# A one-token attention decode on one core: 96 columns for 128 behind the values of three late sets, and the last two projection loads cut by partitions and heads

## The chip, the core and the metric

The kernel runs on one core of one Trainium2 chip. Five engines work side by side and meet at semaphores: TensorE (PE in the profile, with its weight loads as PEld), VectorE (DVE), ScalarE (ACT), GpSimd (POOL) and SyncE (SP), which here only issues transfers. Transfers themselves are carried out by 16 DMA engines. The metric is the device time of one execution in microseconds, a median over several; the profile is one execution taken by the hardware profiler.

## The reference

The input x is 8 tokens of 512 channels. Cut to what matters:

```python
xn = layernorm(x)                                  # no gain, no bias
q  = (xn @ wq)                                     # 8 x 32 heads x 128
k, v = k_cache[:, :, -1024:], v_cache[:, :, -1024:]   # window of 1024 of 4096 keys, 8 kv heads
o  = softmax(q k^T / sqrt(128)) v                  # 4 query heads share one kv head
s  = o.reshape(8, 4096) @ wo
g  = silu((gelu(xn @ w_gate) * (xn @ w_up)) @ w_down)
out = x + s * g
```

All matrices are bf16. The windows of keys and values are 16.8 MB each, and the weights add 13.9 MB (wq and wo 4.2 MB each).

## The kernel before, in words

**Sets.** One kv head of four batch entries is a set; there are 16 of them (`NQ`), sets 2h and 2h+1 belonging to kv head h. A set has 4 x 1024 keys, laid out as 32 chunks (`NCS`) of 128, and 16 query columns (`QC`, four heads by four entries). Its keys are one load of 1 MB, its values another (`load_set`, L122), into a ring of 16 buffers (`NRING`).

**Transfers.** All loads are issued by SP in one order (L176 to L189): the feed-forward weights, wq, the keys of four sets, then for each set q the keys of set q+4 and the values of set q; behind every second set comes `load_wo`, the four heads of the output projection that belong to that kv head, 512 KB as rows of 1 KB (128 partitions, four heads). The values of the last set are loaded as 768 KB and 256 KB. The order at the end is therefore values 12, values 13, projection 24 to 27, values 14, values 15 in two parts, projection 28 to 31. In the built program SP's loads take eight semaphores in turn, and each waits until the load that used its semaphore before, the eighth before it, has landed; a load into the ring also waits until its buffer was read.

**Order on TensorE.** The program is written in a fixed order (L536 to L560). Each step of the loop over q does four quarters `i`, each with eight chunks: transposes of keys two quarters ahead, the values of the set five steps back (`v = q - LAG`), the scores of set q. In between stand the largest score of the set before (`max_all`, L440), which VectorE turns into a shift (L442, L447, L450), and the matmul that subtracts it (`exponentials`, L461), and behind it the exponential on ScalarE (L470). Steps 16 to 20 have no keys any more: they hold the values of sets 11 to 15 alone, with two heads of `project` (L526, four matmuls a head) behind each of the later two quarters at every second step. The four heads 28 to 31 come after the loop (L563), then the gate (L566), four transposes (L569), the sum with x (L571) and the store (L572).

**Values.** `values(g)` (L492) does eight of the 32 chunks of a set. Each matmul takes one chunk of values as weights and the exponentials of that chunk as moving data. It writes `wide` groups of 16 columns: only the first group, the chunk's own, is ever read, and the others are the following chunks' columns, multiplied with the wrong values and left alone. The accumulator `o_ps` has one buffer, so the values of a set start after `normalise` (L511) of the set before has read it.

```python
            wide = VCW if NQ - LAG <= q < NQ - 2 else VC
            wide = wide if n + wide <= NCS else 1
            nc.tensor.matmul(
                o_ps[q][:, 0:wide, :],
                v_sb[q][n],
                pT[q][:, n : n + wide, :],
```

`VC` is 4 (64 columns) and `VCW` is 8 (128 columns); the wide form is used in sets 11, 12 and 13. Where fewer than `wide` chunks are left the matmul has 16 columns.

Of the kernel before, what the change touches and what calls it, by code (L numbers as in the profile page):

```python
# [17 lines left out]
def kernel(  # L18
# [35 lines left out]
    nc = tc.nc  # L54
# [3 lines left out]
    Hkv, Sk, Dh = A_k_cache.shape[1], A_k_cache.shape[2], A_k_cache.shape[3]  # L58
    Hq = A_wq.shape[1] // Dh
    rep = Hq // Hkv  # L60
# [3 lines left out]
    P = nc.NUM_PARTITIONS  # L64
# [9 lines left out]
    NCS = QG * NSC  # L74
    VC = 4
    SC = 8
    VCW = 8
    NRING = 16
    MASK = -1.0e30
    NG = Hkv * B  # L80
    NQ = NG // QG
# [8 lines left out]
    weights = ctx.enter_context(tc.tile_pool(name="weights", bufs=1))  # L90
    ring = ctx.enter_context(tc.tile_pool(name="ring", bufs=NRING))
    consts = ctx.enter_context(tc.tile_pool(name="consts", bufs=1))
# [20 lines left out]
    wo_sb = weights.tile([P, Hq, D], BF16, name="wo_sb")  # L113
# [50 lines left out]
        )  # L164

    def load_wo(hkv):
        nc.sync.dma_start(
            out=wo_sb[:, hkv * rep : (hkv + 1) * rep, :],
            in_=A_wo[hkv * rep * Dh : (hkv + 1) * rep * Dh, :].rearrange(
                "(k p) d -> p k d", p=P  # L170
            ),
        )


    nc.scalar.dma_start(out=x_sb, in_=A_x.flatten_outer_dims())
# [8 lines left out]
    for q in range(NQ):  # L184
        if q + LEAD < NQ:
            load_k(q + LEAD)
        load_v(q)
        if q % SH == SH - 1:
            load_wo(q // SH)  # L189
# [7 lines left out]
        out=ident,  # L197
        in_=ident,
# [14 lines left out]
        out=row_of,  # L213
        in_=row_of,
# [6 lines left out]
    other = consts.tile([QG, QG, rep], BF16, name="other")  # L221
    nc.vector.memset(other, MASK)
    nc.gpsimd.affine_select(
        out=other,
        in_=other,
# [21 lines left out]
    for i in range(2):  # L247
# [3 lines left out]
            out=t[MK : MK + QG, :], in_=other.rearrange("g s j -> g (s j)")  # L251
# [5 lines left out]
        out=spread[MK : MK + QG, :], in_=row_of.rearrange("g e s -> g (e s)")  # L257
# [7 lines left out]
    def keep_busy(n):  # L265
# [12 lines left out]
        out=rstd, in_=mv[:, 1:2], func=ACT.Sqrt, bias=eps_sb, scale=1.0  # L278
# [4 lines left out]
        out=xhat,  # L283
# [208 lines left out]
    def values(g):  # L492
        q, i = divmod(g, NB)
        if i == 0:
            o_ps[q] = ps_o.tile([P, VCW, QC], FP32, name="o_ps")
        for c in range(NSC):
            n = i * NSC + c
            wide = VCW if NQ - LAG <= q < NQ - 2 else VC
            wide = wide if n + wide <= NCS else 1
# [103 lines left out]
```

## Time and profile before

| what | value |
|---|---|
| time, median of 3 runs | 125.16 us (124.97 to 125.5) |
| the profiled execution's own time | 125.26 us |
| its span, first to last instruction | 123.5 us |
| PE busy, share of the span | 107.2 us, 87% |
| DVE busy | 63.3 us, 51% |
| ACT busy | 44.6 us, 36% |
| bytes moved, mean rate | 47.76 MB, 387 GB/s |
| mean granted TensorE clock | 0.986 |

Times in the profile are microseconds from the first instruction. The chain of work that ended last goes back from the last instruction to what released it, or to the instruction before on the same engine. In the chain, a line gives start, length and what ran. In the stretches, each line gives a stretch, its length, the busy time of each engine with its number of instructions, the granted clock, the busy share of the 16 DMA engines and the rate in GB/s. The time from issue to landing of a load is counted from the start of the issue by SP to its last completion event; a load has one such event for each DMA engine that carries a part of it, and a queued load spends most of that time behind the loads before it.

### The profile page before, as it was taken

To read this page: it belongs to the slowest core of one execution; us is meant where nothing else is said; L and a number is where in the kernel's file an instruction comes from. 1 tells how busy PE (TensorE), PEld (TensorE's weight loads), DVE (VectorE), ACT (ScalarE), POOL (GpSimd) and SP (SyncE) were. 2 spreads that over 40 slices of the span, in tenths; PEclk is the share of its full clock that TensorE was granted. 3 is DMA by queue.
4 is the path that set the end of the run, shared out by engine and by line. 5 is a ranking of instruction groups with operands and counts; after the bars stand their busy time and mean duration, and the time that the engine had idled before them with its cause. 6 is when DMAs were issued, how large, how long until landed. Compare 5 with 4: busy or idle time off the path is not lost.

```text
span 123.5 us, 4657 instructions
## 1 busy us (share of the span) xinstructions
PE 107.2 (87%) x2118; PEld 90.0 (73%) x2123; DVE 63.3 (51%) x189; ACT 44.6 (36%) x54; POOL 1.2 (1%) x7
## 2 busy tenths in 40 slices
PE   0999999998999999999999779794999698979980
PEld 0366557456689888899989678793999687868970
DVE  3700001200046888898877576673478385673431
ACT  4000003200027877756655635352536364401000
POOL 3000000000000000000000000000000000000000
PEclk9999999999999999999999999999599999999999
DMA  3999999999999999999999999999999999999600
GB/s 95 413 420 429 426 422 424 424 435 430 416 427 416 432 400 425 422 427 394 434 424 415 418 427 414 414 416 424 419 409 426 424 407 417 415 408 409 237 22 3
DMA packets 10468, 47.76 MB, mean 387 GB/s; under 512 B 832, under 2 KB 4944, under 8 KB 5968
## 3 DMA queue, kind: packets, MB, share of 16 engines
q1 hardware_dynamic: 10432, 47.46, 93.5%
q8 instruction: 16, 0.26, 0.8%
q14 instruction: 4, 0.03, 0.1%
q10 hardware_dynamic: 16, 0.01, 0.0%
HBM read 47.46 MB, written 0.01 MB: 384 GB/s over the span
## 4 chain that ended last, share of the span: by engine, by line
PE 53%; DMA 31%; DVE 10%; issue 4%; POOLq 0%; POOL 0%; ACT 0%; DVEq 0%
DMA ring_sb<-in_A_k_cache_dram 31%; PE idle_ps L267 15%; PE kT_ps L404 10%; PE o_ps L500 8%; PE gu_ps L306 5%; PE sc_ps L421 4%; PE qT_ps L381 3%; PE sc_ps L461 3%; DVE mx L432 2%; DVE kT L411 2%; PE sT_ps L526 1%; PE aux_ps L474 1%; DVE diag L450 1%; DVE diag L447 1%; DVE nm L442 1%
## 5 line engine op out<-in xcount | busy, mean ns | idle before, releaser
L404 PE MATMUL kT_ps<-ident,ring_sb 128*128 128x128 bf16 x512 | 39.6, 221 | 4.8 <-DMA ring_sb<-in_A_k_cache_dram 4.6
L413 ACT COPY kT<-kT_ps 128x1024 bf16<-128x1024 bf16 x32 | 32.4, 1012 | 25.0 <-PE kT_ps L404 24.7
L404 PEld LDWEIGHTS <-ring_sb 128*128 128x128 bf16 x512 | 30.5, 98 | 8.0 <-DMA ring_sb<-in_A_k_cache_dram 5.1
L411 DVE COPY kT<-kT_ps 128x1024 bf16<-128x1024 bf16 x32 | 22.0, 688 | 7.0 <-PE kT_ps L404 6.7
L500 PE MATMUL o_ps<-pT,ring_sb 128*128 128x64 bf16 (+2 forms) x512 | 25.4, 195 | 0.2
L421 PE MATMUL sc_ps<-qT_all,kT 128*128 128x16 bf16 x512 | 22.4, 170 | 1.2 <-ACT pT L470 0.8
L500 PEld LDWEIGHTS <-ring_sb 128*128 128x128 bf16 x512 | 22.3, 99 | 1.1 <-issue 1.0
L267 PE MATMUL idle_ps<-ones_w 128*128 128x512 bf16 x53 | 20.3, 528 | 0.7 <-issue 0.5
L421 PEld LDWEIGHTS <-kT 128*128 128x128 bf16 x512 | 19.3, 96 | 1.8 <-ACT pT L470 0.9
L470 ACT ACTIVATE pT<-sc_ps 128x512 bf16<-128x512 f32 x16 | 9.6, 597 | 18.8 <-PE sc_ps L461 18.8
L432 DVE TENSOR_REDUCE mx<-sc_ps 128x16 f32<-128x512 f32 x16 | 11.1, 692 | 2.6 <-PE sc_ps L421 2.4
L267 PEld LDWEIGHTS <-ones_w 128*128 128x128 bf16 x58 | 6.0, 120 | 7.4 <-issue 6.2
L511 DVE TENSOR_TENSOR oT_all<-o_ps,recip 128x16 bf16<-128x16 f32 x16 | 3.7, 228 | 12.6 <-PE o_ps L500 12.6
L306 PEld LDWEIGHTS <-ring_sb 128*128 128x128 bf16 x112 | 7.5, 161 | 1.8 <-issue 1.8
L306 PE MATMUL gu_ps<-xnT_sb,ring_sb 128*128 128x8 bf16 x112 | 7.2, 201 | 0.3 <-DVE xnT_sb L295 0.3
L461 PE MATMUL sc_ps<-diag,spread 68*128 68x512 bf16 x16 | 6.0, 376 | 1.5 <-DVE diag L450 1.5
L323 DVE TENSOR_SCALAR z<-z 128x112 f32<-128x112 f32 x1 | 0.2, 219 | 13.5 <-ACT z L320 13.5
L526 PE MATMUL sT_ps<-oT_all,wo_sb 128*128 128x8 bf16 x128 | 5.7, 167 | 1.0 <-issue 0.5
L526 PEld LDWEIGHTS <-wo_sb 128*128 128x128 bf16 x128 | 4.9, 97 | 2.2 <-issue 1.6
L474 PE MATMUL aux_ps<-pT,ones_pp 128*128 128x128 bf16 x64 | 6.4, 224 | 0.0
L320 ACT ACTIVATE z<-gu_ps 128x112 f32<-128x112 f32 x1 | 0.3, 265 | 14.8 <-PE gu_ps L306 14.8
L442 DVE TENSOR_REDUCE nm<-aux_ps 16x1 f32<-16x128 f32 x16 | 4.4, 276 | 2.1 <-PE aux_ps L440 1.3
(57 smaller groups left out, 54.3 us busy)
## 6 DMA issues: line engine op xcount, KB each, us to landing
ring_sb<-in_A_k_cache_dram SPq DMA_DIRECT2D x16, 1024.0 KB, 19.2
ring_sb<-in_A_v_cache_dram SPq DMA_DIRECT2D x15, 1024.0 KB, 18.9
ring_sb<-in_A_wq_dram SPq DMA_DIRECT2D x4, 1024.0 KB, 18.9
wo_sb<-in_A_wo_dram SPq DMA_DIRECT2D x8, 512.0 KB, 17.7
ring_sb<-in_B_w_gate_dram SPq DMA_DIRECT2D x2, 896.0 KB, 6.7
ring_sb<-in_B_w_up_dram SPq DMA_DIRECT2D x2, 896.0 KB, 6.7
ring_sb<-in_B_w_down_dram SPq DMA_DIRECT2D x2, 896.0 KB, 12.1
ring_sb<-in_A_v_cache_dram SPq DMA_DIRECT2D x1, 768.0 KB, 14.9
```

The costliest lines, as they stand in the source:

```text
L267: nc.tensor.matmul(idle_ps, ones_w[:, 0:P], ones_w, start=True, stop=True)
L306: nc.tensor.matmul(ffn["gu"][:, j, n % 2, :], up_sb[n][:, i, j::NFC], xnT_sb[:, k, :], start=(n == 0 and j == 0 and i == 0), stop=(k == ND ...
L404: nc.tensor.transpose(kT_ps[:, c * P : (c + 1) * P], k_sb[q][n], ident,)
L411: nc.vector.tensor_copy(out=kT[g], in_=kT_ps)
L413: nc.scalar.copy(out=kT[g], in_=kT_ps)
L421: nc.tensor.matmul(sc[q][:, i * NSC + c, :], kT[g][:, c * P : (c + 1) * P], qT_all[:, b : b + QG, hkv * rep : (hkv + 1) * rep], start=(i = ...
L432: nc.vector.tensor_reduce(out=mx, in_=sc[q].rearrange("p c n -> p n c"), axis=AX.X, op=ALU.max)
L461: nc.tensor.matmul(sc[q], spread, shift[q].unsqueeze(1).to_broadcast([MK + QG, NCS, QC]), start=False, stop=True, skip_group_check=True,)
L470: nc.scalar.activation(out=pT[q], in_=sc[q], func=ACT.Exp, scale=inv_sqrt_dh)
L474: nc.tensor.matmul(sums_ps, ones_pp, pT[q][:, c * SC : (c + 1) * SC, :], start=(c == 0), stop=(c == NCS // SC - 1),)
L500: nc.tensor.matmul(o_ps[q][:, 0:wide, :], v_sb[q][n], pT[q][:, n : n + wide, :], start=(n == 0), stop=(n == NCS - 1), skip_group_check=True,)
L526: nc.tensor.matmul(sT_ps[0][:, d, :], wo_sb[:, h, d * P : (d + 1) * P], oT_all[:, h, :], start=(h == 0 and d == 0), stop=(h == Hq - 1), sk ...
```

## The change

Two things are changed. `VCW` goes from 8 to 6: the values of sets 11, 12 and 13 are multiplied with six chunks of exponentials (96 columns) beside a chunk of values, and the accumulator `o_ps` has six groups. As six chunks fit behind 27 of the 32 chunks and eight behind 25, a set has 27 wide matmuls and 5 of 16 columns in place of 25 and 7.

`load_wo` cuts its last two loads. That of heads 24 to 27 becomes two: partitions 0 to 107, and partitions 108 to 127, each with four heads. That of heads 28 to 31 becomes four: heads 28 to 30 in the same two parts, then head 31 in the same two parts. The bytes are the same. SP issues 55 loads in place of 51, and behind the first part of projection 24 to 27 each load takes another of the eight semaphores, so that it waits for another load than before: the second part waits for keys 14, values 14 for values 10 where it waited for keys 14, the parts of values 15 for keys 15 and values 11 where they waited for values 10 and keys 15, and the four last parts for projection 20 to 23, values 12, values 13 and the first part of projection 24 to 27. The order of instructions on the other engines is the same.

```diff
-    VCW = 8
+    VCW = 6
     NRING = 16
+    CUTS = (0, 108, P)
...
     def load_wo(hkv):
-        nc.sync.dma_start(
-            out=wo_sb[:, hkv * rep : (hkv + 1) * rep, :],
-            in_=A_wo[hkv * rep * Dh : (hkv + 1) * rep * Dh, :].rearrange(
-                "(k p) d -> p k d", p=P
-            ),
-        )
+        h0, h1 = hkv * rep, (hkv + 1) * rep
+        heads = (h0, h1) if hkv < Hkv - 1 else (h0, h1 - 1, h1)
+        cuts = CUTS if hkv >= Hkv - 2 else (0, P)
+        for a, z in zip(heads, heads[1:]):
+            rows = A_wo[a * Dh : z * Dh, :].rearrange("(k p) d -> p k d", p=P)
+            for p0, p1 in zip(cuts, cuts[1:]):
+                nc.sync.dma_start(out=wo_sb[p0:p1, a:z, :], in_=rows[p0:p1, :, :])
```

## The prediction

> **What bounds the kernel now.** I read the profiled execution first by its overview, then by the chain that ended last, then the end by stretches and by its loads. The overview names TensorE, but 87% is a mean over stages:
>
> ```profile
> span 123.5 us, 4657 instructions
> PE 107.2 (87%) x2118; PEld 90.0 (73%) x2123; DVE 63.3 (51%) x189; ACT 44.6 (36%) x54; POOL 1.2 (1%) x7
> GB/s 95 413 420 429 426 422 424 424 435 430 416 427 416 432 400 425 422 427 394 434 424 415 418 427 414 414 416 424 419 409 426 424 407 417 415 408 409 237 22 3
> ```
>
> Rates stay near 420 GB/s until the 37th of 40 slices: there the loads set the pace. The chain shows where that ends:
>
> ```profile
> 83.13 18.51 DMA ring_sb<-in_A_k_cache_dram
> 101.64 0.05 issue
> 101.69 0.62 PE kT_ps L404 x8
> ...
> 109.46 0.89 PE o_ps L500 x16
> 110.35 0.12 PE aux_ps L440
> 110.48 0.02 issue
> 110.50 0.29 DVE nm L442
> ...
> 111.35 0.38 PE sc_ps L461
> 111.72 0.23 PE o_ps L500 x8
> ...
> 112.26 1.50 PE o_ps L500 x24
> ...
> 114.61 1.61 PE o_ps L500 x32
> ...
> 118.23 0.96 PE o_ps L500 x32
> 119.19 0.02 issue
> 119.22 0.24 DVE oT_all L511
> 119.45 0.04 issue
> 119.49 0.56 PE sT_ps L526 x16
> 120.07 0.20 DVE sg L566
> ```
>
> The last keys land at 101.64. From there no load stands in the chain: TensorE works through scores and values, with VectorE's short links between. So a nanosecond saved on TensorE after 101.7 counts, as long as the last loads keep ahead. These are stretches of the end (behind the five engines' busy times: granted clock, DMA share, GB/s) and the last load's size and time to landing:
>
> ```profile
> 114.00:115.00 1.00, 1.00 (x30) 1.00 (x27) 0.54 (x3) 0.00 (x0) 0.00 (x0) 1.00 0.98 375
> 116.00:117.00 1.00, 0.92 (x29) 0.80 (x27) 0.71 (x3) 0.00 (x0) 0.00 (x0) 1.00 0.52 180
> 118.00:119.00 1.00, 1.00 (x35) 1.00 (x34) 0.60 (x3) 0.00 (x0) 0.00 (x0) 1.00 0.04 15
> wo_sb<-in_A_wo_dram SPq DMA_DIRECT2D x1, 512.0 KB, 13.8
> ```
>
> The clock is full. The transfers thin out from 115 on because the DMA engines end apart. The last load is issued at 104.87, so it lands at 118.6-118.7, and its sixteen completion events stand in two groups: nine at 114.9 to 116.4, then 117.8, four at 117.9, 118.2 and 118.6. Its weights are wanted at 119.49: 0.9 us of slack. The cause of the two groups is in the trace's packets: sixteen instruction fetches of 16 KB (about 0.93 us each, with a slow packet behind each), and followed back to back through the packets, eight DMA engines got two each, the other eight none.
>
> **The wide values.** The starts of successive matmuls in sets 11 to 15 stand 55.7 ns apart at 128 columns, 29.2 at 64, 25.3 at 16. Ninety-six columns are not in the trace; they lie between 29.2 and 55.7, and I take the middle, 42.4, since from 64 to 128 a column costs 26.5/64 = 0.414 ns and 2.4 columns a nanosecond fits the full clock.
>
> - Set 13 (and set 12 alike): before 25 x 55.7 + 7 x 25.3 = 1570 ns; after 27 x 42.4 + 5 x 25.3 = 1271. Saved 0.299 us each, all on the chain.
> - Set 11: its first 16 matmuls stand ahead of the transpose of L440, which moves up by 16 x 13.3 = 0.213 us; its operand was ready at 109.29, 0.9 us before it ran. From it the chain goes through VectorE (L442, L447, L450) to L461, 111.35, with TensorE idle for 0.44 us: what the next eight save (0.107) falls into that wait. The last eight are three wide and five narrow in place of one and seven: 254 for 233 ns, 0.021 lost. Saved 0.192.
> - Sum 0.299 + 0.299 + 0.192 = 0.79 us. Bounds: at 29.2 each it would be about 1.7, at 55.7 a loss of 0.06 a set, 0.18 together.
>
> What is late next: the values of set 14 would start at 116.53 - 0.79 = 115.74 (landed 114.8), the first part of values 15 at 117.32 (116.6), chunk 24 at 118.02 (117.3), head 28 at 118.70 (118.6). Head 31 follows twelve matmuls of 25.3 later, at 119.00. So the loads cap the gain near 0.8, even at the cheap bound.
>
> **The divided loads.** The bytes stay; no load stood in the chain after 101.64, so an earlier landing is worth nothing by itself, and what counts is whether head 31's last piece lands after 119.00 and heads 28 to 30 after 118.70. Kilobyte packets start 42.7 ns apart on one DMA engine (32 of them 1.37 us, as the first engine's events at 113.5 and 114.9 show). How 108 and 20 rows fall on the engines is not in the trace: 128 rows give sixteen events, the 8 rows of x eight packets. Bounds: an even share (8 rows an engine as before) lands at 118.6, plus four completion packets of 9 ns; a share on eight engines as for x (16 rows each, 32 more packets in both loads, 2 x 1.37 us) lands at up to 121.3 if late engines are among them. I take a landing of at most 119.0: 108 rows are nearer to 128 than to 8. The cost is then zero, under the cover of the values of sets 14 and 15.
>
> [...]
>
> **Queues.** SP's four more issues cost it under 2 us each (1.33 and 1.64 us for the undivided), and it then waits until 121.18 anyway. Values 14 would be issued once values 10 landed (99.2) in place of 96.83; the first engines reach it at 108.6. Head 31's last piece waits for the first part of projection 24 to 27 (about 112.3), and with an issue and the 1.3 us from issue to landing of the output store it could land from 115; the quickest engines come to it at about 115.5. What covers these is up to 10 us of data queued in front; if that is gone, the piece is late, as in the third rival. Nothing but the store is queued behind it on SP.
>
> **Sum.** The profiled execution took 125.26 us, 123.5 in the span and 1.7 around it, 0.1 above the median of 125.16. 125.26 - 0.79 = 124.47; from the median, 124.4.
>
> **Rivals.**
> - *No change: the pieces fall on the late engines.* [...] For it: half of the engines are late, and which carry which rows the trace does not tell. [...]
> - *Slower: few engines.* The counts seen are 16 and 8; on four engines both pieces split evenly (27 and 5 rows), 96 more packets in each load. Then even a quick engine ends at 115.4 + 8.2 = 123.6 in place of due 119.0: about 129. On eight engines with late ones, 121.3, head 31 1.5 us later than before: 126.7. It decides from a last landing of 119.79, where head 31 begins now. Against: only the smallest load ran on fewer than sixteen.
> - *Slower: each piece pays its own start.* [...] As a mechanism here: three further pieces at the store's 1.3 us in series bring the last landing to 118.6 + 3.9 = 122.5, about 127.9. Against: queued loads follow without a gap (113.5 and 114.9 above are 32 packets apart).
> - *No gain from 96 columns:* at 55.7 a matmul, 125.16 + 0.18 = 125.3. Against: 64 columns do cost less.
>
> **How the numbers follow.** Forecast 124.4 (124.2 to 124.7) 0.58; late engines, 125.1, 0.22; few engines 0.08; piece starts 0.03; dear columns 0.06; the rest 0.03 in between. About 0.5% (0.63 us) is what a measurement of this kernel tells from no change, 124.53 here, and the forecast's own range reaches over it, so 0.04 of it goes to no change: faster 0.54, same 0.35 (with the late engines, the dear columns and the rest), slower 0.11. The range 124.1 to 125.4 takes in the forecast, the late engines and the dear columns; the slower rivals are left out.
>
> **What would show it.** In the changed profile: sets 12 and 13 about 0.3 us shorter each and their matmuls 42 ns apart; L461 of the last set at about 111.1; oT_all of set 15 at 118.4 in place of 119.22; the completion events of the divided loads fewer than 16 and, for head 31, none after 119.0; no DMA in the chain after 101.7. It is wrong if the chain holds wo_sb at its end, or if a wait of values 14 or 15 for its load appears.

## The result: slower by 3.3 us

The changed kernel takes 128.62 us in the median (128.1 to 128.96) against 125.3 us (124.97 to 125.5) for the kernel before: a ratio of 1.0247, 95% interval 1.0206 to 1.0288. The prediction had 124.4, in a range of 124.1 to 125.4. Executions over 1.5% above the fastest of their kernel are left out of the ratios and intervals, here and below, but not out of the medians: the 128.24 us below, for only heads 24 to 27 cut, has one of 168.1 us in it.

The profiled execution of the changed kernel has a span of 126.4 us where the kernel before had 123.5. Its overview, with the granted clock in tenths and the rate by slices:

```profile
span 126.4 us, 4669 instructions
PEclk9995555799999999999999986999999689999855
GB/s 96 415 429 422 428 420 441 417 425 420 433 415 428 428 405 417 423 409 420 428 428 395 430 420 417 418 425 417 411 419 428 419 411 423 268 273 338 195 61 3
```

Up to the 34th slice (107 us) the rates are those of before. Then there are three slices of 268, 273 and 338 GB/s where the kernel before has 415, 408 and 409 in its 35th to 37th slice, so the bytes come in later. (The clock of 0.5 between 10 and 23 us costs nothing: in this stage TensorE waits for weights, and the last keys land at 101.8, where they landed at 101.6 before.)

The end of the chain of the changed kernel, start and length:

```profile
102.76 17.30 DMA ring_sb<-in_A_v_cache_dram
120.06 0.05 issue
120.11 1.81 PE o_ps L504 x32
...
121.94 0.24 DVE oT_all L515
...
122.22 0.58 PE sT_ps L530 x16
...
122.83 0.20 DVE sg L570
...
123.07 0.60 PE sg_ps L573 x4
```

A load now stands in the chain: the 768 KB part of the values of set 15. The timeline of TensorE shows the waits for the values in brackets (start, length, instruction, idle time before it and what ended it):

```profile
114.03 1.42 PE L504 MATMUL o_ps<-pT,ring_sb 128*128 128x96 bf16 x32
116.59 0.40 PE L478 MATMUL aux_ps<-pT,ones_pp 128*128 128x128 bf16 x4 [1.14 <-DVE oT_all L515]
117.50 0.87 PE L504 MATMUL o_ps<-pT,ring_sb 128*128 128x64 bf16 x24 [0.51 <-DMA ring_sb<-in_A_v_cache_dram]
...
120.11 1.80 PE L504 MATMUL o_ps<-pT,ring_sb 128*128 128x64 bf16 x32 [0.87 <-DMA ring_sb<-in_A_v_cache_dram]
```

TensorE comes earlier, as forecast: set 13 begins at 114.03 in place of 114.49, and its 32 matmuls stretch over 1.42 us in place of 1.72. But the values of set 14 land at 117.4 (114.8 before, wanted at 115.74), the two parts of the values of set 15 at 120.1 and 120.8 (116.6 and 117.3; wanted at 117.32 and 118.02), and the last projection piece at 122.3 (118.6; wanted at 119.00). What ended the 1.14 us ahead of L478 is not settled; the values behind it were not there before 117.4 anyway.

Against the forecast span of 123.5 - 0.79 = 122.7: set 15 starts at 120.11 in the chain in place of 118.23 - 0.79 = 117.44 (2.67 us); its matmuls take 1.81 us in place of 0.96 (0.85), and the last matmuls and transposes 0.22 more. With 0.11 less around the store that is the difference of 3.63 us between the two spans.

The stretches in which the bytes were lost (behind the five engines' busy times: granted clock, busy share of the DMA engines, GB/s). First the kernel before:

```profile
108.00:111.00 3.00, 2.39 (x52) 2.17 (x48) 2.08 (x7) 0.38 (x1) 0.00 (x0) 1.00 1.04 417
111.00:114.00 3.00, 2.58 (x52) 2.33 (x52) 1.03 (x5) 0.60 (x1) 0.00 (x0) 1.00 1.02 409
```

Then the changed kernel:

```profile
108.00:111.00 3.00, 2.54 (x62) 2.24 (x61) 2.14 (x8) 0.60 (x1) 0.00 (x0) 1.00 1.04 262
111.00:114.00 3.00, 2.76 (x65) 2.52 (x65) 1.11 (x5) 0.60 (x1) 0.00 (x0) 1.00 1.08 276
117.00:119.00 2.00, 1.50 (x52) 1.51 (x52) 0.73 (x3) 0.00 (x0) 0.00 (x0) 1.00 0.86 221
```

The DMA engines are as busy as before (1.04 and 1.08, against 1.04 and 1.02) and move a third less (262 and 276 GB/s, against 417 and 409). In the trace's packets it is not the new pieces alone that are slow: from 107.7 to 114.3 us packets of 8 KB, which belong to the undivided values, take 414 to 558 ns in the medians by microsecond in place of 309, and kilobyte packets 53 to 72 in place of 46. Between 115 and 116.5 both are back at 309 and 46, and from 117 to 119.2, with the last four pieces in flight, kilobyte packets stretch again (medians of 67 and 58 ns) and so do the 6 KB packets of the values of set 15 (399 and 315 in place of 234). This points to a collision of transfers, which the experiments test. The completion events also show how the rows fall: twelve for 108 rows and ten for 20, besides one at the issue.

### The profile page after: what moved, and what is told of

Same layout as the page of the kernel before. It is cut to its first block, busy times and chain, and to the rows that moved or that the text cites. A ratio compares the mean times of both kernels' runs of the same rounds, so it can differ in the third digit from the quotient of the medians.

```text
span 126.4 us, 4669 instructions
## 1 busy us (share of the span) xinstructions
PE 108.2 (86%) x2123; PEld 91.1 (72%) x2123; DVE 63.2 (50%) x189; ACT 44.6 (35%) x54; POOL 1.2 (1%) x7
## 4 chain that ended last, share of the span: by engine, by line
PE 44%; DMA 43%; DVE 8%; issue 2%; POOLq 0%; POOL 0%; ACT 0%; DVEq 0%; SPq 0%
DMA ring_sb<-in_A_k_cache_dram 30%; PE idle_ps L271 14%; DMA ring_sb<-in_A_v_cache_dram 14%; PE kT_ps L408 9%; PE gu_ps L310 5%; PE o_ps L504 4%; PE sc_ps L425 3%; PE qT_ps L385 3%; DVE mx L436 2%; DVE kT L415 2%; PE sc_ps L465 2%; PE fT_ps L349 1%; PE sT_ps L530 1%; DVE diag L454 1%; DVE diag L451 1%
## 5 line engine op out<-in xcount | busy, mean ns | idle before, releaser
L408 PE MATMUL kT_ps<-ident,ring_sb 128*128 128x128 bf16 x512 | 40.2, 224 | 6.1 <-DMA ring_sb<-in_A_k_cache_dram 6.1
L408 PEld LDWEIGHTS <-ring_sb 128*128 128x128 bf16 x512 | 31.0, 99 | 9.2 <-DMA ring_sb<-in_A_k_cache_dram 6.7
L504 PEld LDWEIGHTS <-ring_sb 128*128 128x128 bf16 x512 | 22.5, 102 | 2.7 <-DMA ring_sb<-in_A_v_cache_dram 1.7
L310 PEld LDWEIGHTS <-ring_sb 128*128 128x128 bf16 x112 | 7.5, 161 | 1.6 <-issue 1.3
L478 PE MATMUL aux_ps<-pT,ones_pp 128*128 128x128 bf16 x64 | 6.7, 231 | 1.1 <-DVE oT_all L515 1.1
L465 PE MATMUL sc_ps<-diag,spread 68*128 68x512 bf16 x16 | 6.0, 376 | 1.6 <-DVE diag L454 1.6
L486 DVE TENSOR_REDUCE recip<-aux_ps 128x16 f32<-128x128 f32 x16 | 4.5, 284 | 1.8 <-PE aux_ps L478 1.8
```

The lines of the kernel that those rows point to most:

```text
L310: nc.tensor.matmul(ffn["gu"][:, j, n % 2, :], up_sb[n][:, i, j::NFC], xnT_sb[:, k, :], start=(n == 0 and j == 0 and i == 0), stop=(k == ND ...
L408: nc.tensor.transpose(kT_ps[:, c * P : (c + 1) * P], k_sb[q][n], ident,)
L465: nc.tensor.matmul(sc[q], spread, shift[q].unsqueeze(1).to_broadcast([MK + QG, NCS, QC]), start=False, stop=True, skip_group_check=True,)
L478: nc.tensor.matmul(sums_ps, ones_pp, pT[q][:, c * SC : (c + 1) * SC, :], start=(c == 0), stop=(c == NCS // SC - 1),)
L504: nc.tensor.matmul(o_ps[q][:, 0:wide, :], v_sb[q][n], pT[q][:, n : n + wide, :], start=(n == 0), stop=(n == NCS - 1), skip_group_check=True,)
```

## The experiments

The theories at first: **L** (lanes): rows that do not fall on the DMA engines as 128 rows do make engines collide. **U** (unequal shares): twelve and ten engines carry what sixteen did. **S** (small pieces): the number of loads and their semaphores. All edits are given against the changed kernel, but for the last one under "Which partitions belong to an engine", which is against the kernel just ahead of it. The bytes loaded are the same in every kernel here, but for the two with further loads, which load 768 KB more.

| kernel | median, us | beside it, kernel before | ratio, 95% interval |
|---|---|---|---|
| changed | 128.62 | 125.3 | 1.0247, 1.0206 to 1.0288 |
| six chunks alone | 124.7 | 125.32 | 0.9951, 0.9926 to 0.9976 |
| division alone | 128.81 | 125.32 | 1.0260, 1.0193 to 1.0327 |
| six chunks, last load by heads alone | 124.67 | 125.32 | 0.9935, 0.9896 to 0.9975 |
| cut at 96 | 127.95 | 125.32 | 1.0186, 1.0132 to 1.0239 |
| whole, source rows 768 bytes apart | 124.63 | 125.58 | 0.9908, 0.9867 to 0.9948 |
| cut at 64, every second source row | 128.36 | 125.58 | 1.0217, 1.0144 to 1.0289 |
| cut at 120 | 127.71 | 125.58 | 1.0173, 1.0096 to 1.0251 |
| only heads 24 to 27 cut at 108 | 128.24 | 125.58 | 1.0162, 1.0059 to 1.0264 |
| only heads 28 to 31 cut at 108 | 125.45 | 125.32 | 0.9986, 0.9955 to 1.0018 |
| further loads into partitions 0 to 31 | 127.18 | 125.32 | 1.0133, 1.0076 to 1.0190 |
| further loads into partitions 64 to 95 | 134.34 | 125.32 | 1.0704, 1.0641 to 1.0766 |
| four chunks, last load by heads alone | 124.48 | 125.32 | 0.9918, 0.9881 to 0.9955 |

### The two parts alone

```diff
-    CUTS = (0, 108, P)
+    CUTS = (0, P)
...
-        heads = (h0, h1) if hkv < Hkv - 1 else (h0, h1 - 1, h1)
+        heads = (h0, h1)
```

> The six chunks alone, loads undivided. All theories say that the columns are worth what the prediction had for them: about 0.8 us, 124.3 to 124.7, with the last projection load landing at 118.6 just ahead of need. If the columns themselves were to blame for the loss, it stays at 128 or more.

Measured: 124.7, ratio 0.9951, a gain of 0.6 us (0.3 to 0.9), within the expectation. The columns are not to blame.

```diff
-    VCW = 6
+    VCW = 8
```

> The division alone, eight chunks as before. If the loads alone make the loss, the values of set 15 land at 120.1 as in the changed kernel, whatever TensorE does before, and the time is 128.1 to 129. If the loss needs both parts (TensorE reaching its loads earlier), it is near 125.3.

Measured: 128.81, the loss of the changed kernel within its interval. The end of this kernel's chain:

```profile
101.86 16.75 DMA ring_sb<-in_A_v_cache_dram
118.61 0.05 issue
118.66 1.31 PE o_ps L504 x24
...
121.16 1.49 PE o_ps L504 x32
```

The chain runs through the values of set 14 here, and TensorE never waits for set 15, whose parts land at 120.9 and 121.5: with eight chunks and a granted clock of 0.5 from 118.9 us on it comes later. The expectation that the values of set 15 land at 120.1 and set the end was too narrow; that the division alone makes the loss stands.

### Pieces, shares or places

Last load by heads alone, and the cut moved to where both parts fall evenly on sixteen engines:

```diff
-    CUTS = (0, 108, P)
+    CUTS = (0, P)
```

> Six chunks, and the last load divided by heads alone (three heads, one head), each piece with all 128 partitions. Theory L (lanes: rows that do not fall on the DMA engines as 128 rows do make engines collide, and every packet in flight takes longer): packets stay at 309 and 46 ns, 124.3 to 124.7. Theory U (unequal shares of the engines): the same. Theory S (small pieces and their semaphores): about half of the loss, 126 or more.

```diff
-    CUTS = (0, 108, P)
+    CUTS = (0, 96, P)
```

> Divided as in the changed kernel but at partition 96: 96 and 32 rows fall evenly on sixteen engines (six and two rows each). Theory L: the rows stand in other places than the same engine's rows of a 128-row load, so 8 KB packets stretch from 309 to 450 ns or more while the pieces run, and the time is 127 to 129. Theory U: even shares, no loss, 124.3 to 124.8. Theory S: as the changed kernel, 128.

Measured: 124.67 with the pieces by heads, their packets at 46 and 309 ns; 127.95 with the cut at 96, 8 KB packets at 444 to 556 ns in the medians between 108 and 115 us. Theory U falls with the second: both parts have sixteen completion events each there (six and two rows an engine), and the time is 3.3 us over that of the kernel divided by heads alone; with nine and two rows on twelve and ten it is 4.0 us over (128.62). Theory S missed with the first, but that kernel has one further piece where the changed one has four, so it tests S in part; the pair of kernels with further loads, below, shows the loss with the number of loads equal. The stretches of the kernel divided by heads alone:

```profile
108.00:111.00 3.00, 2.38 (x58) 2.08 (x55) 2.24 (x8) 0.54 (x1) 0.00 (x0) 1.00 1.04 413
111.00:114.00 3.00, 2.92 (x72) 2.71 (x71) 1.10 (x5) 0.60 (x1) 0.00 (x0) 1.00 1.01 407
```

and of the kernel cut at 96:

```profile
108.00:111.00 3.00, 2.59 (x62) 2.37 (x62) 1.84 (x7) 0.60 (x1) 0.00 (x0) 1.00 1.04 249
111.00:114.00 3.00, 2.37 (x54) 2.02 (x52) 1.31 (x6) 0.60 (x1) 0.00 (x0) 1.00 1.02 264
```

### Reading side or writing side

A divided load changes both what an engine reads and where it writes. One kernel changes only the distance between the source rows. The other changes the partitions and takes every second source row, meant to keep the engines' sources as far apart as before:

```diff
-    CUTS = (0, 108, P)
+    CUTS = (0, P)
...
+            if hkv >= Hkv - 2:
+                rows = bass.AP(A_wo.tensor, a * Dh * D, [[384, P], [Dh * D, z - a], [1, D]])
```

> Undivided partitions, the last load in two by heads as in the kernel divided by heads alone; the rows of the last two loads are read 768 bytes apart in place of 1024, so that sixteen engines read 6 KB apart, as with the cut at 96 (heads 24 to 31 get wrong weights: the last two loads' contents are left out of the computation, their sizes are the same). Theory LS (the collision is on the reading side, by the distance between the engines' addresses): packets stretch as with the cut at 96, about 128. Theory LD (it is on the writing side, by the partitions that an engine writes): 46 and 309 ns, 124.3 to 124.9.

```diff
-    CUTS = (0, 108, P)
+    CUTS = (0, 64, P)
...
-                nc.sync.dma_start(out=wo_sb[p0:p1, a:z, :], in_=rows[p0:p1, :, :])
+                step = P // (p1 - p0)
+                first = p0 * step // P
+                nc.sync.dma_start(out=wo_sb[p0:p1, a:z, :], in_=rows[first:P:step, :, :])
```

> Cut at partition 64: both halves on sixteen engines, four partitions each, and every second row of the source, so that the engines read 8 KB apart as in the undivided load (heads 24 to 31 get their rows in another order: those weights are left out of the computation, sizes the same). Theory LD: packets stretch, 126.5 to 130. Theory LS: 46 and 309 ns, 124.3 to 124.9.

Measured: 124.63 and 128.36. The stretch of the first:

```profile
108.00:111.00 3.00, 2.48 (x54) 2.33 (x51) 1.61 (x5) 0.60 (x1) 0.00 (x0) 0.78 1.01 403
```

and of the second:

```profile
108.00:111.00 3.00, 2.67 (x62) 2.30 (x61) 2.08 (x8) 0.60 (x1) 0.00 (x0) 1.00 1.05 263
```

This speaks for the writing side: source rows 768 bytes apart do no harm (403 GB/s), and halves of 64 partitions do, though their source rows are spread (263 GB/s). It does not settle it, because the distances of 6 and 8 KB in the expectations take the rows of an engine to be neighbours, which the next kernel speaks against. What settles it is the pair behind that one, whose further loads read the same source.

### Which partitions belong to an engine

```diff
-    CUTS = (0, 108, P)
+    CUTS = (0, 120, P)
```

> Cut at partition 120: 120 rows divide by fifteen, eight rows an engine, 8 rows by eight. If an engine's partitions in a 128-row load are eight in a row, the first fifteen engines write where they always do, and only the small piece is out of place: little loss, 124.4 to 125.5. If an engine's partitions in a 128-row load are not eight in a row, it is as bad as the others, 127 to 129.

Measured: 127.71, as bad as expected for partitions that are not eight in a row. That left the place of writing to test by itself, with undivided partitions: the kernel with six chunks and the last load divided by heads alone, and behind the projection loads of kv heads 1, 3 and 5 one further load of 256 KB into a tile that nothing reads. Two kernels write these bytes, from the same source and in the same split (eight completion events each), into two places, partitions 0 to 31 and 64 to 95.

```diff
-    CUTS = (0, 108, P)
+    CUTS = (0, P)
...
+    NP = 4096
+    probe = weights.tile([P, NP], BF16, name="probe")
...
+        if hkv in (1, 3, 5):
+            nc.sync.dma_start(
+                out=probe[0:32, :],
+                in_=bass.AP(A_wo.tensor, 0, [[4 * NP + D, 8], [NP, 4], [1, NP]]),
+            )
```

> [...]

```diff
-                out=probe[0:32, :],
+                out=probe[64:96, :],
```

> [...]

Measured: 127.18 and 134.34, 7.2 us apart for a change of the partitions alone. With partitions 0 to 31, from 25 us on 4062 of 4081 packets of 8 KB take 309 to 313 ns; with 64 to 95, 356 of 4083 take 420 to 700 ns, all of them in three stretches (57 to 63, 82 to 90 and 108 to 116 us), one for each further load. A stretch at the first of them, with partitions 0 to 31:

```profile
57.00:61.00 4.00, 4.00 (x102) 3.76 (x100) 3.31 (x11) 2.53 (x3) 0.00 (x0) 1.00 1.04 424
```

and with partitions 64 to 95, ahead of it, in it and behind it:

```profile
53.00:57.00 4.00, 4.00 (x102) 3.76 (x97) 3.35 (x10) 2.53 (x4) 0.00 (x0) 1.00 1.01 414
58.00:61.00 3.00, 3.00 (x76) 2.76 (x73) 2.35 (x8) 2.16 (x3) 0.00 (x0) 1.00 1.07 237
62.00:66.00 4.00, 2.02 (x47) 1.69 (x44) 1.82 (x7) 1.01 (x1) 0.00 (x0) 1.00 0.98 406
```

So the place that is written decides: source, bytes and split are the same. The stretch at the first load into partitions 64 to 95 lasts some 4 us (58 to 62). The loads into partitions 0 to 31 stretch no packets, but cost time too, 127.18 us against 124.67 without them: the last pieces' completion events are three at 115.2 to 116.4, then a group at 117.9 to 119.9, then 121.4 and 121.5. Eight engines got three times four packets of 8 KB more, which start 306 ns apart in the trace of the kernel before, by estimate 3.7 us. This fits two late engines among the eight (117.8 + 3.7 = 121.5); then the late engines are not simply the other eight.

No trace here names the DMA engine of a packet, so which partitions an engine writes in a 128-row load is not shown, nor why one place is slow and the other not. Shown is that 32 partitions from 0 on stretch nothing, that 32 from 64 on stretch every 8 KB packet that began between 58 and 62 us (97 packets, the least 448 ns), and that 120 rows, by their events on fifteen engines, with the other 8 on eight, take the rate to 288 GB/s between 108 and 111 us.

### Where in the changed kernel

```diff
-        cuts = CUTS if hkv >= Hkv - 2 else (0, P)
+        cuts = CUTS if hkv == Hkv - 2 else (0, P)
```

> Only the load of heads 24 to 27 divided at 108; the last one by heads alone. In the changed kernel packets are stretched twice, from 107.7 to 114.5 and from 117 to 119.5. Theory L in either form: the first stretch stays, the values of set 15 land at about 119 and the time is 127 to 128. If the loss came mostly from the four last pieces, it is under 125.5.

```diff
-        cuts = CUTS if hkv >= Hkv - 2 else (0, P)
+        cuts = CUTS if hkv == Hkv - 1 else (0, P)
```

> Only the last load divided at 108 (and by heads), the load of heads 24 to 27 whole. Packets stretch only from about 114 on, when most of values 15 is in. If the loss follows the data still in flight beside the pieces, it is small: 124.7 to 126. If each divided load costs the same, half of the loss: 126.5.

Measured: 128.24 with the first load divided (about 127.6 by the ratio), and 125.45 with the last. Against 124.67 without a cut, the last load's pieces cost about 0.8 us and the first's the greater part, though its interval is wide (1.0162, 1.0059 to 1.0264) and only its times are shown here, not its packets. With only the last one divided, 8 KB packets stay at 309 up to 114 us, and the end waits for the pieces themselves, in the chain of that kernel:

```profile
106.00 13.43 DMA wo_sb<-in_A_wo_dram
119.43 0.14 issue
119.57 0.44 PE sT_ps L530 x12
```

That the loss follows the data in flight beside the pieces fits both times.

### Fewer columns still

```diff
-    VCW = 6
+    VCW = 4
...
-    CUTS = (0, 108, P)
+    CUTS = (0, P)
```

> Four chunks (64 columns) in all sets, no cut by partitions, last load in two by heads: TensorE would save 1.7 us against the kernel before, but the last loads land at 118.6 as before and hold the end: 124.2 to 124.6, no more than 0.4 better than six chunks with the same loads (124.67).

Measured: 124.48, ratio 0.9918 (0.9881 to 0.9955). It is faster than the kernel before, by under 1%, and than the changed kernel; from six chunks with the same loads (0.9935, 0.9896 to 0.9975) it can't be told apart. In its chain TensorE waits 0.22 us behind the matmuls of set 13, where the kernel with six chunks and the same loads has 0.02; what it waits for the profile does not show:

```profile
114.02 0.94 PE o_ps L504 x32
114.97 0.22 issue
115.18 0.40 PE aux_ps L478 x4
```

## Why the prediction was wrong

- **The wide values: right.** Matmuls of ninety-six columns stand 42.3 ns apart at a granted clock of 1.00 (42.4 predicted, the middle of 29.2 and 55.7), set 13 went from 1.61 to 1.31 us on the chain where no load is late (in the kernel divided by heads alone), and the six chunks alone gained 0.6 us (0.3 to 0.9) where 0.79 was forecast. L461 of the last set, L465 in the changed kernel, came at 111.16, predicted 111.1.
- **The divided loads: the step that failed.** "The cost is then zero, under the cover of the values of sets 14 and 15." Both bounds counted packets at 42.7 ns and asked only how many an engine gets. The price of the packet itself changed, for all loads in flight: the 127 packets of 8 KB that began between 108 and 114 us took 381 to 605 ns, in the median 509, where all took 309 in the kernel before. What I named as cover was the victim: the values of sets 14 and 15 came 2.6 and 3.5 us later, and TensorE waited for them, which was my own sign of being wrong. The bound of 121.3 for the last landing was passed as well (122.3).
- **The rival of few engines** named times on both sides of the measured one (126.7 and about 129) by luck, since its mechanism was wrong: not four or eight engines carried the pieces but, by the completion events, twelve and ten, and the cut at 96, with all sixteen, is 3.3 us behind the kernel divided by heads alone (127.95 against 124.67).
- **The rival of late engines** had a part of it: five of the twelve events and three of the ten stand in the later group. No run shows the 125.1 that the chances give it, nor what late engines alone are worth; with these shares the changed kernel took 128.62.
- **Each piece paying its own start**: the one further piece of the kernel divided by heads alone cost nothing that shows (124.67 against 124.7). Dividing by partitions did cost, and what these runs speak for is where the pieces write, not their start: with the number of loads equal, the further loads into partitions 64 to 95 took 134.34 us, and those into 0 to 31 took 127.18.
- **Queues:** the issues came later than worked out, values 14 at 102.1 in place of 99.2, because the issue of the second part held SP for 5.05 us and not under 2, and the last piece at 114.7 in place of about 112.3. The DMA engines stayed busy (1.04 and 1.08 between 108 and 114 us), so no load is seen to be late by its issue.
- **Not forecast at all:** TensorE's clock. In the profiled execution it ran set 15 at 53 ns a matmul in place of 29, at a granted clock of 0.5, which with the last transposes is 1.1 of the 3.63 us.

## What to carry to other kernels

Before counting bytes and engines, ask where a transfer into fewer than 128 partitions writes: the same 768 KB in three loads took 7.2 us more in partitions 64 to 95 than in 0 to 31, and the last two loads cut at partition 108, 96, 64 or 120 cost some 3 us or more (128.62, 127.95, 128.36 and 127.71 us against 124.67). Cutting along the free axis (by heads here) left the packets at 46 and 309 ns and cost nothing that these runs can tell (124.67 us against 124.7). When the DMA engines are as busy as before and move fewer bytes (1.04 and 262 GB/s here, in place of 1.04 and 417), look at the time of one packet, and at that of the other loads' packets first.

## What the runs showed of the hardware that was not expected

- A load of 256 KB into partitions 64 to 95, with eight completion events, slowed every 8 KB packet in flight from 309 ns to a median of 586 (all 97 that began between 58 and 62 us, the least 448), and the rate from 414 to 237 GB/s; the same bytes into partitions 0 to 31 slowed none. The kernels with three such loads differ by 7.2 us.
- A wait near the end can cost twice: in the changed kernel the granted clock was 0.51 between 119 and 122 us, behind waits of 1.14 and 0.51 us, and 64-column matmuls stood 53 ns apart in place of 29. It does not always: in the kernel cut at 120 the waits were 1.43 and 0.82 us, the clock stayed full between 117 and 122 us, and set 15 ran at 29 ns a matmul. What decides it the runs do not show.
- The sixteen instruction fetches of this program go, followed through the packets, to eight DMA engines, two each. Seven engines end the last load some 2.5 us behind the others: in the kernel before, its completion events are nine at 114.9 to 116.4 and seven at 117.8 to 118.6.
